# Chunked attention and a channel mixer: the first batch's front in another order, softmax by minima with exponentials from PSUM, v in fewer transfers

## The chip, the cores and the metric

The kernel runs on one core of a Trainium2 chip. The metric is the device time of one execution in microseconds (us), the median of three runs. The core has engines that run side by side, each through its own list of instructions in order: TensorE (PE, matmuls into PSUM; its weight loads are listed as PEld), VectorE (DVE), ScalarE (ACT), GpSimd (POOL), and SyncE (SP), whose queue issues all DMA transfers of this kernel. Semaphores make an instruction wait for one of another engine or for a transfer. SBUF is the working memory, PSUM holds the results of matmuls in eight banks of 128 x 512 floats.

## The reference

Four batches, 8 heads, 768 positions, head size 64. Attention runs over chunks of 32 queries, each with 8 memory keys and up to 56 keys around the chunk; a low-rank mix over the sequence and a two-layer feed-forward follow. All inputs are float32.

```python
for c in range(nc):                      # 24 chunks
    l_start, r_end = max(0, 32 * c - 16), min(S, 32 * c + 40)
    k_full = concat([mem_k, k[:, :, l_start:r_end]], axis=2)
    v_full = concat([mem_v, v[:, :, l_start:r_end]], axis=2)
    scores = scale * q_c @ k_full.T
    scores = scores - max(scores, axis=-1)
    a = exp(scores)
    a = a / (sum(a, axis=-1) + 1e-09)
    out[:, :, 32 * c:32 * c + 32] = a @ v_full
...
xt = x.transpose(0, 2, 1)                # x: out with the heads side by side, 768 x 512
h = xt @ U @ V                           # U 768 x 32, V 32 x 768
u = x + h.transpose(0, 2, 1)
return u + maximum(u @ w_ch1, 0) @ w_ch2 # 512 -> 2048 -> 512
```

## The kernel before

The weights U, V, w1 and w2 come as 64-bit floats and are read as pairs of words. A class `Words` turns them into a float32 value on the chip: `begin` (ScalarE, one instruction for each transferred half), `bits`, `low` and `join` (VectorE). A weight block f (16 of them, 128 hidden columns each) has two chunks, 2f for w1 and 2f+1 for w2. `finish` splits a chunk's value into a high part (a ScalarE copy, L322) and a low part (a VectorE subtraction, L323), since each product of the feed-forward runs as three matmul passes. The generator `stream` (L332) walks through all chunks; one call of `advance(1)` is one step of it: begin of the next chunk with bits of this one and finish of the one before, then low, then join.

Attention works in three steps T of 256 query positions (`NP` = 3). For each T:

- `regroup` (L398, VectorE) reorders raw k and q; `k_part` and `q_part` transpose them on PE and copy them to `kall` and `qt` (L472 to L480 and L492). `kall` holds the windows of two T, so k_part(2) writes the half of T=0 and the last edge of T=1.
- `s_turn` (L508) computes the scores of one T into two PSUM banks with 128 small matmuls.
- `s_weights` (L515) takes them out, for each bank: a memset for positions beyond the ends, a maximum over each window of 64 columns (L530), a subtraction into `pt` (L531), both on VectorE, and one exponential over 512 columns on ScalarE (L534).
- `s_sums` (L536) sums and inverts; `t_part` (L550) transposes the probabilities on PE and copies them out on ScalarE (L558); `av_part` (L560) multiplies with v and, on VectorE, with the inverse sums (L579), which gives x.

For batch 0 these parts are called in an order written out by hand in `attention` (from L601), with `collect` (x times U), `spread_v`, `turn_x` and calls of `advance` among them. In this front, PE, VectorE, ScalarE and SP all keep the order in which the code calls them (`manual_schedule`); `keep_clock` adds matmuls on zeros. PSUM banks are taken by `bank` in a fixed cycle of seven (`cyc`, L98), so the n-th request waits until the reader of the (n-7)-th is done. After the front, g (x times U, collected) is split (L780, L781), joined with V into u (`join_uT`, L824; `join_uT1`, L855), and the feed-forward begins: `both_blocks` (L946) runs the hidden blocks f of both halves of batch 0, while VectorE still decodes weights; it needs chunks 2f and 2f+1 for block f. The attention of batches 1 to 3 is placed among the feed-forward of the batch before, there with `s_part` and the planner's order.

Loads follow a list, `LOADS`, all on the SP queue: `t` are k and q of one T (6 transfers for T=0, 4 each for the others), `mk` mem_k, `uv` U and V (4), `mv` mem_v into a small tile (2), `v0` to `v2` the windows of v of one T (8 transfers, of 56 rows and one head each, and 2 for the ends of the sequence), `mm` copies of the small tile into every window of all three homes (6), `w0` to `w2` three weight blocks (3 each).

```python
LOADS = 't0 mk t1 t2 uv mv v0 mm v1 w0 v2 w1 w2'
cyc = ["a", "h", "a", "o0", "a", "h", "o1"]
```

## Time and profile before

| | |
|---|---|
| median of 3 runs | 707.15 us (703.69, 707.15, 709.41) |
| the profiled execution | 707.29 us |
| its span, first to last instruction | 705.5 us |
| mean granted clock of PE | 0.973 |
| bytes moved by DMA | 79.35 MB |

In a table of stretches each row starts with the stretch in us and its length, then gives busy time and instructions of PE, PEld, DVE, ACT and POOL, the granted clock of PE (1.00 is full), the mean busy share of the 16 DMA engines and what they moved in GB/s. In a timeline a row gives start, duration, engine, line, operation, out<-in by the program's names, shapes, the number of instructions merged into the row, and in brackets the idle time before it with what ended it. Instructions that follow each other on one engine overlap in their durations, so the distance of two starts is what one costs. SPq rows are issues of transfers, not the transfers.

### The profile page before, as it was taken

The numbers are of one execution on the slowest core, as the hardware profiler recorded it, in microseconds if no ns is written. First come the engines' busy times: TensorE is split into PE (matmuls) and PEld (weight loads), VectorE is DVE, ScalarE is ACT, GpSimd is POOL, SyncE is SP. The second block draws the span as 40 slices with busy tenths as digits, with TensorE's granted clock in tenths as the row PEclk, the third lists the DMA queues.
The fourth block names the chain that finished last, engine by engine and source line by source line (L and its number), as shares of the span: only waits on it lengthen the run. The fifth ranks groups of instructions, "written<-read, shape, count | busy, mean of one in ns | idle before, by whom it ended". The sixth has DMA issues, their size and how long they took to land.

```text
span 705.5 us, 14740 instructions
## 1 busy us (share of the span) xinstructions
PE 670.0 (95%) x6284; PEld 583.1 (83%) x6284; DVE 319.1 (45%) x652; ACT 190.0 (27%) x470; POOL 10.1 (1%) x35
## 2 busy tenths in 40 slices
PE   7786999999977899999999999999999999999997
PEld 4465999998956489998988998898978999989996
DVE  5868989999673622316413222316313321112111
ACT  4534434333541113332211223222211211111110
POOL 2000000000000000000000000000000000000000
PEclk9997999999997789999999999999999999999999
DMA  8696444414453096412511178412411042214211
GB/s 228 158 279 234 149 150 150 155 45 131 129 143 111 33 231 170 110 41 89 131 32 61 31 220 197 121 46 88 128 34 59 32 129 65 60 31 134 74 47 45
DMA packets 103658, 79.35 MB, mean 112 GB/s; under 512 B 49480, under 2 KB 83400, under 8 KB 103592
## 3 DMA queue, kind: packets, MB, share of 16 engines
q1 hardware_dynamic: 103592, 78.40, 38.7%
q8 instruction: 49, 0.80, 0.5%
q14 instruction: 17, 0.14, 0.1%
HBM read 66.72 MB, written 10.49 MB: 109 GB/s over the span
## 4 chain that ended last, share of the span: by engine, by line
PE 85%; DVE 8%; DMA 2%; issue 2%; ACT 1%; SPq 1%; POOL 0%; DVEq 0%; ACTq 0%; POOLq 0%
PE ps_h L889 37%; PE acc L932 21%; PE acc L937 11%; PE ps_a L570 2%; PE ps_a L508 2%; PE ps_a L932 2%; PE ps_a L449 2%; DMA w1l<-w1ld 2%; PE ps_a L555 1%; PE acc L590 1%; PE ps_a L937 1%; DVE mx L530 1%; DVE pt L531 1%; PE ps_a L874 1%; PE ps_a L596 1%
## 5 line engine op out<-in xcount | busy, mean ns | idle before, releaser
L896 DVE SCALAR_TENSOR_TENSOR hl<-ps_h,hh 128x384 fp32r<-128x384 f32 x127 | 70.5, 556 | 252.1 <-ACT hh L895 251.4
L889 PE MATMUL ps_h<-uh,w1h 128*128 128x384 f32 x508 | 173.6, 343 | 8.0 <-ACT w1h L322 7.3
L889 PE MATMUL ps_h<-ul,w1h 128*128 128x384 f32 x508 | 172.3, 340 | 0.2 <-DVE ul L877 0.2
L932 PE MATMUL acc<-w,hh 128*128 128x512 f32 x594 | 156.4, 397 | 0.8 <-DVE x L903 0.8
L895 ACT ACTIVATE hh<-ps_h 128x384 fp32r<-128x384 f32 x127 | 62.5, 492 | 304.7 <-PE ps_h L889 304.7
L932 PEld LDWEIGHTS acc<-w,hh 128*128 128x128 f32 x594 | 109.2, 188 | 23.2 <-DVE x L903 1.2
L889 PE MATMUL ps_h<-uh,w1l 128*128 128x384 f32 x508 | 111.7, 341 | 1.7 <-DMA w1l<-w1ld 1.7
L889 PEld LDWEIGHTS ps_h<-uh,w1h 128*128 128x128 f32 x508 | 96.3, 190 | 13.5 <-ACT w1h L322 8.0
L889 PEld LDWEIGHTS ps_h<-ul,w1h 128*128 128x128 f32 x508 | 96.6, 190 | 3.0 <-DVE ul L877 0.7
L889 PEld LDWEIGHTS ps_h<-uh,w1l 128*128 128x128 f32 x508 | 92.1, 192 | 3.1 <-DMA w1l<-w1ld 2.3
L937 PE MATMUL acc<-w,hl 128*128 128x512 f32 x297 | 84.4, 391 | 0.0
L937 PEld LDWEIGHTS acc<-w,hl 128*128 128x128 f32 x297 | 55.7, 188 | 11.9
L932 PE MATMUL acc<-w2last,hh 128*128 128x512 f32 x90 | 25.7, 413 | 0.0
L794 DVE TENSOR_TENSOR x<-ps_a,x 128x512 f32<-128x512 f32 x24 | 15.6, 686 | 22.1 <-PE ps_a L792 22.1
L472 ACT COPY kall<-ps_a 128x256 f32<-128x256 f32 x40 | 16.9, 422 | 26.5 <-PE ps_a L449 26.5
L903 DVE TENSOR_TENSOR x<-acc,x 128x512 f32<-128x512 f32 x24 | 15.5, 685 | 18.2 <-PE acc L937 14.4
L508 PE MATMUL ps_a<-kall,qt 64*32 64x64 f32 x1344 | 19.4, 224 | 3.8 <-issue 3.5
L508 PEld LDWEIGHTS ps_a<-kall,qt 64*32 64x32 f32 x1344 | 16.8, 105 | 7.2 <-issue 6.6
L534 ACT ACTIVATE pt<-pt 128x512 f32<-128x512 f32 x24 | 14.6, 630 | 26.3 <-DVE pt L531 26.3
L932 PEld LDWEIGHTS acc<-w2last,hh 128*128 128x128 f32 x90 | 17.3, 198 | 3.9 <-issue 0.8
L194 DVE SCALAR_TENSOR_TENSOR vb<-vb 128x512 int32<-128x512 int32 x29 | 20.1, 692 | 0.9
L210 DVE TENSOR_TENSOR vb<-vb 128x512 f32<-128x512 f32 x29 | 20.0, 691 | 0.8
(186 smaller groups left out, 639.2 us busy)
## 6 DMA issues: line engine op xcount, KB each, us to landing
w1l<-w1ld SPq DMA_DIRECT2D x99, 256.0 KB
rw<-in_moe_w_ch_dram SPq DMA_DIRECT2D x14, 512.0 KB
qraw<-in_q_dram SPq DMA_DIRECT2D x24, 256.0 KB
out_dram<-x SPq DMA_DIRECT2D x24, 256.0 KB
vb<-in_v_dram SPq DMA_DIRECT2D x56, 98.0 KB
raw<-in_moe_w_ch_dram SPq DMA_DIRECT2D x20, 256.0 KB
kraw<-in_k_dram SPq DMA_DIRECT2D x16, 256.0 KB
rw<-in_moe_w_ch_dram SPq DMA_DIRECT2D x16, 256.0 KB
```

The source lines that it names most:

```text
L194: nc.vector.scalar_tensor_tensor(out=ti, in0=yi, scalar=-2 ** 31, in1=ti, op0=ALU.bitwise_and, op1=ALU.bitwise_or,)
L210: self.adder.tensor_tensor(out=t, in0=t, in1=y, op=ALU.add)
L472: copy(out=kt[:, p, :, :, m:m + w], in_=psv[:, q_])
L508: nc.tensor.matmul(out=psv[s][CK * i:CK * i + CK, t, p % 2, p // 2, :], lhsT=qt[p // 2][rows, p % 2, NI * t + i, :], rhs=kall[rows, NB * ( ...
L534: nc.scalar.activation(out=pt, in_=pt, func=AF.Exp, scale=scale)
L794: nc.vector.tensor_tensor(out=x, in0=hp, in1=x, op=ALU.add)
L889: nc.tensor.matmul(out=ph[:, :TOK], lhsT=w[:, c, :], rhs=u[c], start=(m == 0), stop=(m + 1 == len(parts)),)
L895: nc.scalar.activation(out=hh, in_=ph[:, :TOK], func=AF.Relu)
L896: nc.vector.scalar_tensor_tensor(out=hl, in0=ph[:, :TOK], scalar=0.0, in1=hh.bitcast(F32), op0=ALU.max, op1=ALU.subtract,)
L903: nc.vector.tensor_tensor(out=x, in0=bank, in1=x, op=ALU.add)
L932: nc.tensor.matmul(out=acc[tt], lhsT=h[:, sl], rhs=w, start=(begins and m == 0), stop=False,)
L937: nc.tensor.matmul(out=acc[tt], lhsT=hl[:, sl], rhs=w2h[f], start=False, stop=ends is not None)
```

## The change

The sign of the scores is turned: q is copied with a factor of -scale, so the memory holds negative scaled scores. `s_weights` becomes `s_min` (memsets with +3e38 and a minimum for each window, on VectorE) and `s_exp`: for each of the 8 windows of a bank one exponential straight from PSUM, exp(min - score), with the minimum as the bias operand. The subtraction on VectorE is gone, and the bank is held until the exponentials have read it. This holds for all batches.

In the front of batch 0, U's begin and a first `advance(1)` come ahead of k_part(2); U's other steps, the exponentials, the sums and the transposes move to later places, each `s_exp` behind other work; steps of the weight stream are spread over the front, 8 in all where there were 5. V's words get a home of their own instead of one of the three scratch pairs.

The homes of v for T=0 and 1 become one tile of 16 windows. `load_v_span` loads it with one transfer for each head and half (15 windows instead of 7 and 8), 10 transfers where there were 18; the copies of mem_v fill all windows of a tile in one transfer for each half. In the list of loads, mem_v moves ahead of t1, and w0 ahead of all of v.

```diff
-LOADS = 't0 mk t1 t2 uv mv v0 mm v1 w0 v2 w1 w2'
+LOADS = 't0 mk mv t1 t2 uv m0 w0 va m1 vb w1 w2'
...
-    vbs = [const.tile([P, NB, 4 * D], F32, name=f"vb{n}") for n in range(2)]
+    vb01 = const.tile([P, 2 * NB, 4 * D], F32, name="vb01")
+    vbs = [vb01[:, NB * n:NB * n + NB] for n in range(2)]
...
+                for j in range(4):
+                    rows = vv[b, g, CK * n0 - LEFT:CK * n0 - LEFT + NW - NM, j]
+                    step, count = rows.ap[0]
+                    nc.sync.dma_start(
+                        out=home[r0:r0 + NW - NM, n0 - m0:n1 - m0, D * j:D * j + D],
+                        in_=bass.AP(rows.tensor, rows.offset, [[step, count], [CK * step, n1 - n0], rows.ap[1]]),
+                    )
...
-                (nc.vector.tensor_copy if b == 0 and T == 0 else nc.scalar.copy)(
-                    out=qt[:, q_].rearrange("c i (n r) -> c r i n", r=2), in_=psv[:, q_],
-                )
+                to, src = qt[:, q_].rearrange("c i (n r) -> c r i n", r=2), psv[:, q_]
+                if b == 0 and T == 0:
+                    nc.vector.tensor_scalar(out=to, in0=src, scalar1=-scale, scalar2=None, op0=ALU.mult)
+                else:
+                    nc.scalar.mul(out=to, in_=src, mul=-scale)
...
-                nc.vector.tensor_reduce(out=mx, in_=sc, axis=AX.X, op=ALU.max)
-                nc.vector.tensor_tensor(
-                    out=ptv, in0=sc, in1=mx[:, :, None].broadcast_to([P, 8, NW]), op=ALU.subtract,
-                )
-                nc.scalar.activation(out=pt, in_=pt, func=AF.Exp, scale=scale)
+                nc.vector.tensor_reduce(out=mn, in_=sc, axis=AX.X, op=ALU.min)
+                mins[T, s] = sc, mn
+
+        def s_exp(T, s):
...
+            for a in range(8):
+                nc.scalar.activation(
+                    out=pt[:, NW * a:NW * a + NW], in_=sc[:, a], func=AF.Exp, bias=mn[:, a:a + 1], scale=-1.0,
+                )
```

The order of batch 0's front after the change, from the first scores on (each line ends at a `yield`):

```python
keep_clock(GAP[0]); sc = s_turn(0); q_part(1, *); s_min(0, *sc)
regroup(qraw, qn, "qn", 2); u_words.begin(); advance(1); k_part(2, *); u_words: bits, low, join; s_exp(0, *)
keep_clock(GAP[1]); sc = s_turn(1); q_part(2, *); s_min(1, *sc); s_sums(0); t_part(0, *)
s_exp(1, *); advance(2); sc = s_turn(2); s_min(2, *sc)
keep_clock(GAP[2]); v_words.begin(); s_sums(1); t_part(1, *); s_exp(2, *); advance(1); av_part(0); v_words: bits, low, join; collect(0, 1)
t_part(2, *); av_part(1); s_sums(2); spread_v; collect(2, 3); turn_x; advance(1)
keep_clock(GAP[3]); av_part(2); advance(3); keep_clock(CHAIN[0]); collect(4, 5); turn_x1 twice
```

Before, it was:

```python
keep_clock(GAP[0]); sc = s_turn(0); q_part(1, *); s_weights(0, *sc)
regroup(qraw, qn, "qn", 2); k_part(2, *); s_sums(0); t_part(0, *)
keep_clock(GAP[1]); sc = s_turn(1); q_part(2, *); s_weights(1, *sc)
sc = s_turn(2); u_words: begin, bits, low, join; t_part(1, *); s_weights(2, *sc); s_sums(1)
keep_clock(GAP[2]); av_part(0); v_words: begin, bits, low, join; s_sums(2); t_part(2, *); collect(0, 1)
av_part(1); spread_v; advance(1); collect(2, 3); turn_x; advance(3)
keep_clock(GAP[3]); av_part(2); advance(1); keep_clock(CHAIN[0]); collect(4, 5); turn_x1 twice
```

More of the change, by code (lines that the diff above doesn't have):

```diff
@@ L17 @@
 U32 = mybir.dt.uint32
-NEG = -3.0e38
+FAR = 3.0e38
 NSLOT = 23
@@ L183, in begin @@
                 return
-            self.y, self.t = work_pair()
+            if self.home is None:
+                self.y, self.t = work_pair()
+            else:
+                both = const.tile([P, 2, 256], F32, name="dec", tag=self.home)
+                self.y, self.t = both[:, 0, :], both[:, 1, :]
             for raw, c in self.pieces():
@@ L546, in s_part @@
         def s_part(T):
-            s_weights(T, *s_turn(T))
+            s_min(T, *s_turn(T))
+            for s in range(2):
+                s_exp(T, s)
             s_sums(T)
@@ L652, in attention @@
                 q_part(1, h)
-            s_weights(0, *sc)
+            s_min(0, *sc)
             yield
             regroup(qraw, qn, "qn", 2)
+            u_words.begin()
+            advance(1)
             for h in two:
                 k_part(2, h)
-            s_sums(0)
-            for s in two:
-                t_part(0, s)
-            yield
-            keep_clock(GAP[1])
-            sc = s_turn(1)
-            for h in two:
-                q_part(2, h)
-            s_weights(1, *sc)
-            yield
-            sc = s_turn(2)
-            u_words.begin()
             u_words.bits()
@@ L677, in attention @@
             for s in two:
-                t_part(1, s)
-            s_weights(2, *sc)
-            s_sums(1)
+                s_exp(0, s)
+            yield
+            keep_clock(GAP[1])
+            sc = s_turn(1)
+            for h in two:
+                q_part(2, h)
+            s_min(1, *sc)
+            s_sums(0)
+            for s in two:
+                t_part(0, s)
+            yield
+            for s in two:
+                s_exp(1, s)
+            advance(2)
+            sc = s_turn(2)
+            s_min(2, *sc)
             yield
             keep_clock(GAP[2])
+            v_words.begin()
+            s_sums(1)
+            for s in two:
+                t_part(1, s)
+            for s in two:
+                s_exp(2, s)
+            advance(1)
             av_part(0)
-            v_words.begin()
             v_words.bits()
@@ L687, in attention @@
             val = v_words.join()
-            s_sums(2)
-            for s in two:
-                t_part(2, s)
             for t in two:
@@ L693, in attention @@
             yield
+            for s in two:
+                t_part(2, s)
             av_part(1)
+            s_sums(2)
             spread_v(val)
-            advance(1)
             for t in two:
@@ L700, in attention @@
             early = turn_x()
-            advance(3)
+            advance(1)
             yield
@@ L704, in attention @@
             av_part(2)
-            advance(1)
+            advance(3)
             keep_clock(CHAIN[0])
@@ L721, in attention @@
                 clear_v()
-                for home in vbs[:2]:
-                    mem_v(home)
+                mem_v(vb01)
             yield
@@ L742, in attention @@
                         clear_v()
-                        for home in vbs[:2]:
-                            mem_v(home)
+                        mem_v(vb01)
                         yield
```

55 lines of the change are left out of this document (37 added, 18 removed).

## The prediction

> **What bounds the kernel now.** I read the page first (span and shares), then the table of stretches, one for each stage: PE, weight loads, VectorE, ScalarE, POOL busy, then granted clock, DMA share, GB/s.
>
> ```profile
> span 705.5 us, 14740 instructions
> PE 670.0 (95%) x6284; PEld 583.1 (83%) x6284; DVE 319.1 (45%) x652; ACT 190.0 (27%) x470; POOL 10.1 (1%) x35
> ...
> 0.00:62.00 62.00, 43.72 (x940) 29.58 (x941) 45.73 (x108) 27.84 (x79) 4.88 (x19) 0.93 0.81 234
> 62.00:176.00 114.00, 113.68 (x567) 103.02 (x565) 105.04 (x207) 45.50 (x96) 0.00 (x0) 0.98 0.41 132
> 260.00:705.00 445.00, 440.05 (x3736) 393.21 (x3736) 122.09 (x240) 89.90 (x219) 2.63 (x8) 1.00 0.32 88
> ```
>
> The profiled execution took 707.29 us, 1.8 more than its span and 0.1 above the median of 707.15. From 62 to 176 PE is busy 113.7 of 114 us, from 260 on 440 of 445. So the front, up to the first matmuls of f=1 at 60.78, is a lump that everything behind it follows: a front shorter by x is worth x. VectorE decodes weights beside PE until 176 (105 of 114 us busy), nearly as full, so it cannot repay a late start either.
>
> Next the chain of waits, the timeline of VectorE, ScalarE and the SP queue, for the front.
>
> ```profile
> 18.59 0.43 PE ps_a L116 x2
> 20.64 0.68 DVE mx L530
> 60.78 4.21 PE ps_h L889 x12
> ...
> 15.13 0.69 ACT L492 COPY qt<-ps_a 128x256 f32<-128x256 f32 x2
> 17.25 0.63 ACT L534 ACTIVATE pt<-pt 128x512 f32<-128x512 f32 x1 [0.92 <-DVE pt L531]
> 17.79 0.38 ACT L472 COPY kall<-ps_h 128x256 f32<-128x256 f32 x1
> 18.69 0.24 ACT L476 COPY kall<-ps_h 128x48 f32<-128x48 f32 x1
> 18.78 0.26 ACT L480 COPY kall<-tail 128x32 f32<-128x32 f32 x1
> 20.03 0.68 ACT L558 COPY pt<-ps_a 128x512 f32<-128x512 f32 x1
> 43.54 0.44 ACT L186 ACTIVATE dec<-rw 128x256 f32<-128x256 f32 x1 [2.14 <-DMA rw<-in_moe_w_ch_dram]
> 44.23 0.43 ACT L186 ACTIVATE dec<-raw 128x256 f32<-128x256 f32 x1 [0.24 <-DMA raw<-in_moe_w_ch_dram]
> ...
> 22.67 0.69 DVE L531 TENSOR_TENSOR pt<-acc,mx 128x512 f32<-128x512 f32 x1
> 29.73 1.27 DVE L539 TENSOR_REDUCE rs<-pt 128x8 f32<-128x512 f32 x2
> 39.70 0.41 DVE L579 TENSOR_TENSOR x<-ps_h,rs 128x256 f32<-128x256 f32 x1
> 46.04 1.42 DVE L579 TENSOR_TENSOR x<-ps_a,rs 128x256 f32<-128x256 f32 x4 [1.63 <-PE ps_a L570]
> 49.24 0.42 DVE L781 TENSOR_TENSOR g<-acc,g 32x256 fp32r<-32x256 f32 x1
> 54.17 0.42 DVE L200 TENSOR_SCALAR dec<-dec 128x512 int32<-128x512 int32 x1
> 57.62 0.55 DVE L896 SCALAR_TENSOR_TENSOR hl<-ps_a,hh 128x384 fp32r<-128x384 f32 x1
> ...
> 11.14 2.22 SPq L226 DMA_DIRECT2D vraw<-in_moe_V_dram  x3
> 13.40 0.68 SPq L620 DMA_DIRECT2D mv<-in_mem_v_dram  x2
> 19.55 3.04 SPq L413 DMA_DIRECT2D vb<-mv  x4
> 30.56 0.45 SPq L281 DMA_DIRECT2D rw<-in_moe_w_ch_dram  x1
> 40.32 0.82 SPq L281 DMA_DIRECT2D rw<-in_moe_w_ch_dram  x1
> 41.18 0.46 SPq L281 DMA_DIRECT2D raw<-in_moe_w_ch_dram  x1
> ```
>
> Two places matter. Scores, subtraction and exp wait for each other on VectorE and ScalarE from 14 to 32. And behind the joined u (54.17) VectorE decodes 3.45 us for chunk 1 and 2, then 0.55 for hl, then chunk 2 again, while PE stands idle until 60.78.
>
> **The change part by part.**
>
> Subtractions. Six in the front at 0.69 us (22.67): VectorE is freed of 4.1 us, 1.4 in each score step.
>
> Exponentials. Each 512-column exp becomes eight of 64 columns with a bias per partition. No row has that operand. Low bound: the 512-column exp starts 17.25 and the next instruction 17.79, 0.54; the 48-column copy lets the next one start 0.09 later (18.69, 18.78), so 464 columns fewer cost 0.40 less than a 512-column copy's 0.49 and a 64-column exp takes about 0.13. High bound: no overlap at all, the 0.26 of the 32-column copy. I take 0.15, near the exp's own row. Sixteen make 2.4 us of ScalarE where 1.1 stood, 48 make 7.2 for 3.2: ScalarE gains 4.0 (3.0 to 9.3). [...]
>
> mem_v ahead. Its two loads move from 13.40 to before the loads of t1, 0.68 of SP issue. The queue is full there (DMA share 1.04 in the table below), so the k of T=1 comes 0 to 0.7 later; I take 0.3.
>
> First weights ahead, and the wait they bring. SP now ends the loads of V at 13.4+0.3. Then two copies of mv over 16 blocks instead of 8: 0.76 each (3.04/4) if the size is free, 1.5 if not; I take 1.0, so w0 is issued at 15.7 and its second half at 16.2. From issue to use such a half took 43.54-40.32 = 3.2 and 44.23-41.18 = 3.05 us. So it is there at 19.2 (18.3 to 20.5). In the new order ScalarE runs u's first step and then `advance(1)`, the begin of chunk 0, before the copies of k_part(2) and before the exponentials. It gets there at 16.4 (the q copies of T=1 end 15.13+0.69 = 15.8, 0.3 later now, 0.3 for u) and stands 2.8 us. Behind it on the same engine: 0.43 for the second half, twelve copies (17.79 to 20.03, 2.24), eight exps (1.2), which free the bank that s_turn(1) needs (seven banks in turn). Sum 19.2+0.43+2.24+1.2 = 23.1. s_turn(1) takes 1.6 (from the warming matmuls' end at 19.02 to its reader at 20.64) and ends at 24.7: 4.1 late.
>
> Making it up. VectorE's part of T=1 and 2 is shorter by 2.8, but ScalarE is the bound now: the q copies wait for s_turn(1) and their transposes until 25.6 and take 1.1, two pT copies 1.0, sixteen exps 2.4, which brings 30.1; s_turn(2) starts at half of those, 28.9, and ends at 30.5; minima with their memsets 1.7, sums 1.7 (1.27 and two small steps), join 0.7, four products 1.4 give x of T=0 at 36. Then two collects 2.0, two pT 1.1, av 1.45 and products 1.4: x of T=1 ends near 41.5 against 40.1. Collects, 24 transposes, av(2) and products follow as before: x of T=2 ends at 49.0 against 47.4 (46.04+1.42), 1.6 late.
>
> Decode ahead. Eight steps of the stream run before "joined" instead of five. Chunk 0's bits, low part and join (3.0 us) now lie where VectorE waits. But `advance(3)` puts low, join, bits and rest of chunk 1 (3.45, the block from 54.17 to 57.62) between x and g: g starts at 49.0+3.45 = 52.5 instead of 49.24. From g to the end of ul is 54.17-49.24 = 4.9, so 57.4 against 54.17. Then hl (its matmuls and relu first, 1.8), low and join of chunk 2 (1.9) and the w1h copy with its wait 0.7: f=1 starts at 61.8 to 62.3. I take 62.3, 1.5 late.
>
> v in fewer transfers.
>
> ```profile
> 15.00:20.00 5.00, 3.58 (x123) 2.67 (x123) 4.44 (x10) 4.08 (x17) 0.00 (x0) 1.00 0.68 155
> 30.00:35.00 5.00, 3.46 (x8) 1.23 (x8) 4.79 (x14) 1.86 (x4) 0.00 (x0) 0.74 0.80 205
> ```
>
> Ten issues fewer, the same bytes, hidden: v moves behind w0, and av(0) needs all of va (15 blocks of 56 rows of 256 B, eight times, 1.7 MB). At the 155 to 205 GB/s of two stretches of v loads, from 19 on, that is 27 to 30; av(0) comes at 32. If that cover goes, each us late is a us. vb has until 46, w1 until 42. The multiplication by -scale rides on copies of the same size, the sentinel and the tile for V's words change no time: 0.
>
> The clock. In windows of 3.41 us:
>
> ```profile
> 5.07:8.48 3.41, 3.18 (x22) 2.16 (x20) 1.28 (x3) 2.15 (x10) 0.00 (x0) 1.00 1.04 287
> 8.48:11.90 3.42, 1.72 (x10) 1.00 (x10) 2.59 (x9) 1.86 (x10) 0.00 (x0) 1.00 1.07 317
> 28.97:32.38 3.41, 1.50 (x9) 1.06 (x10) 3.31 (x10) 2.01 (x4) 0.00 (x0) 1.00 0.72 157
> 32.38:35.79 3.41, 3.41 (x17) 0.73 (x24) 3.27 (x9) 0.00 (x0) 0.00 (x0) 0.50 0.90 264
> 63.10:66.51 3.41, 3.41 (x14) 3.41 (x14) 2.57 (x5) 1.70 (x3) 0.00 (x0) 0.50 0.94 303
> 66.51:69.92 3.41, 3.41 (x22) 3.12 (x21) 2.40 (x6) 1.73 (x5) 0.00 (x0) 1.00 0.07 26
> 213.28:216.70 3.42, 1.42 (x103) 1.38 (x102) 0.68 (x3) 0.00 (x0) 0.40 (x1) 1.00 0.75 259
> 233.76:237.18 3.42, 1.33 (x4) 0.24 (x2) 0.68 (x1) 1.17 (x2) 0.00 (x0) 1.00 0.00 0
> ```
>
> A window with PE busy 1.50 or less is followed by half clock, one with 1.72 is not; full clock returns after a full window (63.10, then 66.51). [...] PE, idle from 17.2 to 23.0 in my schedule, has one whole window empty, well under 1.50 busy, so s_turn(1) and what follows run at half clock. Its four steps between (s_turn, q, pT, s_turn, some 5 us) cost up to 2.9 where PE ends last, nothing where ScalarE does: I take 1.5. At f=1 the idle time shrinks from 6.5 to some 4 us; half clock from 60.78 to 66.51 cost 2.9, I take back 1.0 (0 to 1.4).
>
> Batches 1 to 3. The exps cost ScalarE 1.3 us more per step. From 260 on the waits of PE are one line:
>
> ```profile
> PE ps_h L889 <- DMA w1l<-w1ld: 1.7, 2, 1.0
> ```
>
> ScalarE is busy 90 of 445 us there, and no transpose of the probabilities waits for it. Cover: PE has the feed-forward to do. Without it each of nine steps would cost 1.3, less 1.4 of VectorE. Batch 1 around 195 to 250 has little cover, but the two nearly cancel: 0 (-1 to +1).
>
> Sum: +1.5 (f=1 later) +1.5 (half clock early) -1.0 (less of it at f=1) +0 = +2.0; 707.3+2.0 = **709.3 us**.
>
> **The rivals.**
>
> *Slower by over 1%.* ScalarE as the front's bound with the clock low throughout. Place: 17 to 58. If one exp takes 0.25, near its high bound (+2.1), and PE, always waiting a little for ScalarE, never fills a window before g, its 8 us of transposes, av and collects on the path run twice as long, +4 more. 709.3+6.1 = 715. It decides from 0.2 per exp with half clock beyond 30. For it: no row excludes that price. Against: collects at 32.38 filled a window at once.
>
> *Faster.* The half clocks of batch 1 (two windows, 1.42 and 1.33 busy) hang on where windows fall. Idle time there is 2 to 3 us; moved by half a window it parts into two windows above 1.72 each. Both gone returns some 10 us: 699. For it: three runs differ by 5.7. Against: all lie above 703.
>
> *It changes nothing.* w0 lands before ScalarE asks (copies of mv at 0.7, half 2.8) and exps cost 0.13: f=1 at 60, cold a little less, 705.5. For it: bounds from rows. Against: even then issue at 15.2 plus 3.05 is 18.2, after 16.4.
>
> **How the numbers follow.** Forecast (706.5 to 713) 0.52, slower rival 0.20, faster 0.13, nothing (703 to 706.5) 0.15. 1%, about what a measurement can tell here, is 7.1 us: under 700.1 only the faster rival, 0.13; over 714.2 the slower, 0.20; between 0.67. The range 701 to 716 leaves out the better part of the faster rival and the tail of the slower one.
>
> **What would show it.** Right: ScalarE idle for about 2.8 us before the second begin of chunk 0, released by the DMA of w0; s_turn(1) after 23; half clock in the twenties; no VectorE decode of chunk 1 behind ul; f=1 at 61 to 64. Wrong: begin of chunk 0 without a wait, 64-column exps 0.2 apart or more, av(0) released by a v transfer, f=1 before 60, or a second half clock missing in batch 1.

## The result and the profile after

| | before | after |
|---|---|---|
| median of 20 runs each | 707.27 us | 712.57 us |
| lowest and highest | 703.69 to 711.97 us | 707.34 to 716.51 us |
| after : before | | 1.0073, 95% interval 1.0053 to 1.0094 |
| span of the profiled execution | 705.5 us | 710.3 us |

The kernel became slower by 5.3 us: by less than one per cent, and more than the measurement's error. First the head of the page and the sums by engine, as the changed kernel has them.

```profile
span 710.3 us, 14864 instructions
PE 674.2 (95%) x6284; PEld 585.7 (82%) x6284; DVE 304.8 (43%) x628; ACT 215.3 (30%) x638; POOL 10.6 (1%) x35
```

VectorE gave up 14 us and ScalarE took on 25, as the exchange of a subtraction for seven more exponentials says; PE stays the bound. Where the span grew is read by cutting both executions at the same points of the work. The cuts here are the starts of the 4th, 28th, 37th, 65th, 73rd and 91st Relu of the feed-forward on ScalarE. Table of stretches of the kernel before, without its second row and its last:

```profile
0.00:76.03 76.03, 57.75 (x1006) 42.61 (x1007) 57.69 (x130) 34.13 (x92) 4.88 (x19) 0.91 0.76 220
...
180.26:267.26 87.00, 75.74 (x1060) 59.84 (x1059) 42.58 (x91) 27.95 (x82) 2.62 (x8) 0.86 0.50 135
267.26:409.56 142.30, 142.30 (x1475) 126.36 (x1474) 46.98 (x95) 33.48 (x83) 2.02 (x6) 1.00 0.28 78
409.56:445.56 36.00, 34.96 (x192) 31.84 (x191) 7.53 (x17) 10.18 (x34) 0.00 (x0) 1.00 0.83 208
445.56:539.88 94.32, 94.32 (x1217) 82.45 (x1216) 33.37 (x71) 22.79 (x54) 0.61 (x2) 1.00 0.28 81
```

And the same work in the changed kernel:

```profile
0.00:81.42 81.42, 60.39 (x1006) 44.41 (x1007) 53.93 (x124) 40.10 (x135) 4.85 (x19) 0.90 0.73 205
...
185.66:268.20 82.54, 74.42 (x1060) 58.82 (x1059) 39.76 (x85) 34.37 (x124) 2.02 (x6) 0.88 0.52 136
268.20:411.19 142.99, 142.76 (x1475) 126.52 (x1474) 43.09 (x89) 39.94 (x124) 2.02 (x6) 1.00 0.29 81
411.19:449.26 38.07, 36.02 (x187) 32.62 (x186) 7.53 (x17) 9.44 (x33) 0.00 (x0) 0.96 0.79 197
449.26:544.99 95.73, 95.73 (x1222) 83.28 (x1221) 29.48 (x65) 29.96 (x97) 0.61 (x2) 1.00 0.28 80
```

Call them A (the front), B (the attention of batch 1), the long one, C (the loads of batch 2) and D. A grew by 5.4 us, B shrank by 4.5, the long one, C and D grew by 0.7, 2.1 and 1.4; the stretches left out are equal or 0.3 shorter. That is the 4.8 us of the span. In these two executions the front lost what the whole lost, and behind it a gain and a loss of four to five us cancel. Of B's gain 3.1 us are idle time of PE (11.3 us before, 8.1 after), the rest is work at a higher clock (75.74 and 74.42). One execution of each is little to go by: the twenty runs of one kernel lie 8 to 9 us apart, so a few us in a stretch are shown only where other runs repeat them.

The front, in the timeline of the changed kernel:

```profile
13.73 1.66 SPq L418 DMA_DIRECT2D vb<-mv  x2
15.43 1.60 SPq L286 DMA_DIRECT2D rw<-in_moe_w_ch_dram  x1
17.09 2.50 SPq L286 DMA_DIRECT2D raw<-in_moe_w_ch_dram  x1
...
15.49 0.38 ACT L191 ACTIVATE dec<-uarea 128x192 f32<-128x192 f32 x1 [0.26 <-DMA uarea<-in_moe_U_dram]
21.70 0.43 ACT L191 ACTIVATE dec<-rw 128x256 f32<-128x256 f32 x1 [5.84 <-DMA rw<-in_moe_w_ch_dram]
22.49 0.43 ACT L191 ACTIVATE dec<-raw 128x256 f32<-128x256 f32 x1 [0.36 <-DMA raw<-in_moe_w_ch_dram]
22.83 0.35 ACT L500 COPY kall<-ps_h 128x256 f32<-128x256 f32 x1
25.07 1.82 ACT L567 ACTIVATE pt<-ps_h,mn 128x64 f32<-128x64 f32 x8
26.65 0.44 ACT L567 ACTIVATE pt<-ps_a,mn 128x64 f32<-128x64 f32 x1
...
24.01 0.31 PE L538 MATMUL ps_h<-kall,qt 64*32 64x64 f32 x1 [8.09 <-ACT kall L504]
66.36 1.65 PE L936 MATMUL ps_h<-uh,w1h 128*128 128x384 f32 x4 [3.68 <-ACT w1h L327]
...
37.95 0.42 DVE L616 TENSOR_TENSOR x<-ps_a,rs 128x256 f32<-128x256 f32 x1
45.01 0.42 DVE L616 TENSOR_TENSOR x<-ps_h,rs 128x256 f32<-128x256 f32 x1
52.77 1.42 DVE L616 TENSOR_TENSOR x<-ps_a,rs 128x256 f32<-128x256 f32 x4 [2.78 <-PE ps_a L607]
54.11 0.42 DVE L205 TENSOR_SCALAR dec<-dec 128x512 int32<-128x512 int32 x1
57.67 0.42 DVE L828 TENSOR_TENSOR g<-acc,g 32x256 fp32r<-32x256 f32 x1
```

ScalarE finishes U's begin at 15.9 and then stands 5.84 us for w0, and 0.36 for its second half. Everything behind it waits in order: the copies of k_part(2) from 22.83, and for these PE, which stands 8.09 us and goes on with s_turn(1) at 24.01, ahead of the exponentials from 25.07; in the kernel before, its warming matmuls ended at 19.02 and s_turn(1) followed at once. One exponential follows the next after (26.65-25.07)/8 = 0.197 us. f=1 starts at 66.36 instead of 60.78.

Why w0 is late is seen in the landings, which the profiler records as semaphore events of each transfer (us; worked out from the trace):

```
kernel, transfer                           issued   landed   between
before  copies of mv, 64 KB, first two      19.55    22.82      3.27
                                            20.44    23.94      3.50
after   copies of mv, 128 KB, both          13.73    19.04      5.31
                                            14.69    21.44      6.75
after   w0, the two halves of w1's block    15.43    21.68      6.25
                                            17.09    22.47      5.38
after   last part of v for T=0 and 1        31.06    35.90      4.84
```

w0's halves land right behind the two copies, 5.4 to 6.3 us after issue instead of about 3.1. Part of this is SP itself: the two issues last 1.60 and 2.50 us, where the same two take 0.45 and 0.46 in the kernel before, and 1.58 and 0.47 in the first experiment, which has no copies in front of them. So the copies go with the standing of the second; what holds SP is not shown. And v, which is behind w0, is complete at 35.9 and not between 27 and 30.

The clock, in stretches of 3.41 us, and one of 5 us for the transfers. In the two traces, before and after, the stretches at half clock lasted 3.41, 6.83, 10.24 or 13.65 us, but for one that the end of each execution cuts off (worked out from the trace); a window is a stretch of 3.41 us on that grid.

```profile
15.00:20.00 5.00, 0.92 (x7) 0.32 (x5) 2.97 (x9) 0.61 (x2) 0.35 (x1) 1.00 0.61 94
17.02:20.43 3.41, 0.00 (x0) 0.00 (x0) 1.05 (x3) 0.00 (x0) 0.35 (x1) 1.00 0.72 113
20.43:23.84 3.41, 0.00 (x0) 0.00 (x0) 0.00 (x0) 1.78 (x8) 0.00 (x0) 0.50 0.97 289
23.84:27.25 3.41, 3.24 (x132) 3.07 (x133) 1.02 (x2) 3.41 (x21) 0.40 (x1) 0.50 0.60 94
426.62:430.03 3.41, 1.38 (x8) 1.30 (x9) 1.70 (x5) 0.38 (x1) 0.00 (x0) 1.00 0.75 146
430.03:433.44 3.41, 3.41 (x11) 2.92 (x10) 0.56 (x1) 0.69 (x3) 0.00 (x0) 0.50 0.94 239
44.32:47.73 3.41, 3.29 (x10) 1.21 (x5) 3.31 (x10) 2.06 (x6) 0.00 (x0) 0.50 0.96 333
```

PE does nothing from 17.02 to 23.84, and the clock is at half until 27.25, over all of s_turn(1) that was left; a window from 44.32, with collects and transposes of x, is at half clock too. In stretch C a window with 1.38 us of work is followed by one at half clock; the kernel before has none in C. From 15 to 20 us the transfers move 94 GB/s with the engines 0.61 busy; in the kernel before it was 155. In the trace the first copy of mv, to 8 partitions, raised its semaphore in 9 steps, from 15.00 to 19.04 us, and the first half of w0, to 128 partitions, in 16, from 20.50 to 21.68.

### The profile page after: what moved, and what is told of

The parts are those of the page before. It is cut to its first block, busy times and chain, and to the rows that moved or that the text cites. A ratio compares the mean times of both kernels' runs of the same rounds, so it can differ in the third digit from the quotient of the medians.

```text
span 710.3 us, 14864 instructions
## 1 busy us (share of the span) xinstructions
PE 674.2 (95%) x6284; PEld 585.7 (82%) x6284; DVE 304.8 (43%) x628; ACT 215.3 (30%) x638; POOL 10.6 (1%) x35
## 3 DMA queue, kind: packets, MB, share of 16 engines
q1 hardware_dynamic: 103416, 78.40, 38.7%
## 4 chain that ended last, share of the span: by engine, by line
PE 83%; DVE 5%; DMA 4%; SPq 4%; ACT 1%; issue 1%; DVEq 0%; ACTq 0%
PE ps_h L936 36%; PE acc L979 21%; PE acc L984 10%; DMA w1l<-w1ld 3%; PE ps_a L607 2%; PE ps_a L979 2%; PE ps_a L538 2%; PE ps_a L477 2%; SPq L440 1%; PE ps_a L592 1%; PE ps_a L984 1%; PE ps_a L633 1%; PE ps_a L921 1%; PE acc L627 1%; DVE x L841 1%
## 5 line engine op out<-in xcount | busy, mean ns | idle before, releaser
L979 PE MATMUL acc<-w,hh 128*128 128x512 f32 x594 | 158.4, 401 | 0.3 <-DVE x L950 0.3
L567 ACT ACTIVATE pt<-ps_a,mn 128x64 f32<-128x64 f32 x168 | 36.4, 389 | 17.8 <-DVE mn L555 15.4
L574 DVE TENSOR_REDUCE rs<-pt 128x8 f32<-128x512 f32 x24 | 16.3, 686 | 15.6 <-ACT pt L567 15.6
L616 DVE TENSOR_TENSOR x<-ps_a,rs 128x256 f32<-128x256 f32 x44 | 15.7, 410 | 11.2 <-PE ps_a L607 7.4
```

Of the source, the lines that this page charges most:

```text
L567: nc.scalar.activation(out=pt[:, NW * a:NW * a + NW], in_=sc[:, a], func=AF.Exp, bias=mn[:, a:a + 1], scale=-1.0,)
L574: nc.vector.tensor_reduce(out=rs[:, :, :, :, s].rearrange("n t g k -> n t k g"), in_=pts[T, s].rearrange("n (t k g w) -> n t k g w", t=2, ...
L616: nc.vector.tensor_tensor(out=x[:, 4 * D * g:4 * D * g + 4 * D].rearrange("n (j d) -> n j d", d=D), in0=psv[g][:, t], in1=rs[:, t, g].rear ...
L979: nc.tensor.matmul(out=acc[tt], lhsT=h[:, sl], rhs=w, start=(begins and m == 0), stop=False,)
```

## The experiments

Each kernel was timed in five rounds beside the kernel before on the same chip. The table gives the ratio of its time to that of the kernel before with the interval, the start of f=1 and the lengths of A, B, C and D in its profiled execution (us). One execution was profiled of each, so these lengths carry the scatter of one run; that of the loads alone was the fastest of its twelve (707.68 us, their median 711.50).

| kernel | ratio | interval | f=1 | A | B | C | D |
|---|---|---|---|---|---|---|---|
| before | 1 | | 60.78 | 76.03 | 87.00 | 36.00 | 94.32 |
| after | 1.0073 | 1.0053 to 1.0094 | 66.36 | 81.42 | 82.54 | 38.07 | 95.73 |
| w0 ahead of the copies | 1.0053 | 1.0030 to 1.0076 | 62.43 | 76.61 | 85.63 | 38.53 | 95.70 |
| begin later | 1.0076 | 1.0050 to 1.0102 | 64.29 | 78.48 | 85.70 | 38.71 | 95.70 |
| one exponential | 1.0069 | 1.0042 to 1.0095 | 67.97 | 82.47 | 81.00 | 35.89 | 95.58 |
| before, loads alone | 1.0040 | 1.0013 to 1.0068 | 64.76 | 78.72 | 81.41 | 37.13 | 94.43 |
| before, softmax alone | 0.9982 | 0.9961 to 1.0003 | 61.34 | 76.61 | 85.05 | 35.56 | 94.43 |
| steps as before | 1.0104 | 1.0081 to 1.0127 | 66.14 | 80.17 | 87.12 | 36.18 | 95.81 |
| same, v ahead of w0 | 1.0041 | 1.0018 to 1.0064 | 61.49 | 75.72 | 86.69 | 37.75 | 95.70 |
| small copies later | 1.0026 | 0.9995 to 1.0056 | 66.74 | 80.71 | 85.15 | 35.66 | 95.58 |
| front rebuilt | 0.9981 | 0.9957 to 1.0005 | 61.59 | 76.87 | 83.16 | 35.89 | 94.35 |
| same, v by T | 0.9958 | 0.9924 to 0.9991 | 64.44 | 78.97 | 79.08 | 36.19 | 94.46 |
| same, av(2) earlier | 0.9952 | 0.9926 to 0.9978 | 62.49 | 77.01 | 79.56 | 38.55 | 95.65 |
| same, v of T=1 ahead of w0 | 0.9898 | 0.9873 to 0.9923 | 60.59 | 74.67 | 78.34 | 35.55 | 95.61 |

### w0 ahead of the copies

```diff
-LOADS = 't0 mk mv t1 t2 uv m0 w0 va m1 vb w1 w2'
+LOADS = 't0 mk mv t1 t2 uv w0 m0 va m1 vb w1 w2'
```

> The changed kernel with the first weights w0 loaded ahead of the two 16-block copies of mem_v instead of behind them; nothing else moves. Theory (ScalarE stands for w0, and w0 stands behind the copies): w0's halves are issued at about 13.7 and 14.5 and are there by 18, ScalarE's two waits for them shrink from 5.84+0.36 to under 2.5 us, s_turn(1) ends near 22.5 instead of 26.05, f=1 starts 2 to 4 us earlier than 66.36, and the time is 0.997 to 1.004 of the kernel before (after: 1.0073). Rival A (the eight small exponentials and the half clock carry the loss): the waits shrink but f=1 stays within 1 us of 66.4, ratio 1.006 to 1.009. Rival B (the transfers are only full: whatever is behind the copies comes late): the copies land later, v with them, av(0) waits for v by 2 us or more, ratio 1.005 or more.

ScalarE's timeline of this run:

```profile
18.32 0.44 ACT L191 ACTIVATE dec<-rw 128x256 f32<-128x256 f32 x1 [1.99 <-DMA rw<-in_moe_w_ch_dram]
18.99 0.43 ACT L191 ACTIVATE dec<-raw 128x256 f32<-128x256 f32 x1 [0.24 <-DMA raw<-in_moe_w_ch_dram]
```

The waits fell from 6.2 to 2.2 us, s_turn(1) ended at 22.3 and f=1 came 3.9 us earlier, as the theory had it: the copies held w0. Of the front's 5.4 us all but 0.6 was gone. PE stood 1.2 us for v, less than rival B asked. The ratio stayed above the theory's range, at 1.0053; in the profiled execution B was 3.1 us longer than in the changed kernel, and the timing does not tell the two kernels apart.

### The begin later on ScalarE

```diff
             u_words.begin()
-            advance(1)
...
             for s in two:
                 s_exp(0, s)
+            advance(1)
             yield
```

> The changed kernel with ScalarE's first step of the weight stream put behind the copies of k_part(2) and the exponentials of T=0 instead of ahead of them; loads and the number of steps unchanged. Theory (order on ScalarE): k_part(2) and the exponentials no longer wait for w0, s_turn(1) ends by 21 instead of 26.05, f=1 starts 3 to 5 us earlier than 66.36, ratio to the kernel before 0.996 to 1.003. Rival A (exponentials and clock): ratio 1.006 to 1.009. Rival C (the wait only moves: ScalarE now stands for w0 ahead of the q copies of T=2 and the exponentials of T=1, or av(0) stands for v that lands at 28 to 36 anyway): x of T=0 not before 36, f=1 within 1.5 us of 66.4, ratio 1.005 to 1.008.

PE's waits from 12 to 46 us (in total, times, longest):

```profile
PE ps_a L607 <- DMA vb<-in_v_dram: 3.3, 4, 1.0
PE ps_a L592 <- ACT pt L567: 1.9, 1, 1.9
PE ps_a L607 <- DVE dec L215: 1.6, 1, 1.6
```

s_turn(1) ended at 19.2, seven us earlier than in the changed kernel, and x of T=0 came at 38.5, no earlier at all: av(0) began at 28.6 and went on to 37.1, since it stood again and again for parts of v, at half clock between (0.31 us a matmul at 30.64, as at 24.01 in the changed kernel, and 0.22 there at 36.71, at full clock). (The 1.6 us put down to a step of the decoding are v's too: that step ends at 30.1, a part of v landed at 30.47, and PE went on at 30.56.) This is rival C in its place and its ratio: behind the wait for w0 stood the wait for v. That f=1 came 2.1 us earlier is more than the 1.5 that it allowed. It was won later: x of T=1 came 0.4 us earlier, x of T=2 1.6, and between them the changed kernel has its collects and transposes at half clock.

### One exponential again

```diff
                 nc.vector.tensor_reduce(out=mn, in_=sc, axis=AX.X, op=ALU.min)
-                mins[T, s] = sc, mn
+                nc.vector.tensor_tensor(out=pt..., in0=sc, in1=mn[:, :, None]..., op=ALU.subtract)
...
-            for a in range(8):
-                nc.scalar.activation(out=pt[...], in_=sc[:, a], func=AF.Exp, bias=mn[:, a:a + 1], scale=-1.0)
+            nc.scalar.activation(out=pt, in_=pt, func=AF.Exp, scale=-1.0)
```

> The changed kernel with the softmax of before (row extreme, subtraction on VectorE, one exponential of 512 columns) in the new order and with the new loads. Theory: ScalarE loses 0.8 to 1.0 us of exponentials per bank in the front (eight at 0.197 against one of about 0.5 to 0.6), VectorE gains 0.69 per bank; the wait for w0 stays 5 to 6 us, so f=1 moves by at most 1.5 us from 66.36 and the ratio to the kernel before is 1.004 to 1.009. Rival A (the eight exponentials are the cost): f=1 3 us or more earlier and ratio 1.000 to 1.003.

Ratio 1.0069, as the theory said: the eight exponentials are not the loss. f=1 came 1.6 us later, a little outside the expected 1.5; in that run ScalarE stood 7.45 us for w0, also more than the 5 to 6 expected.

### The softmax alone, in the kernel before

```diff
-                    out=qt[...], in_=psv[:, q_],
+                    nc.scalar.mul(out=to, in_=src, mul=-scale)
...
-                nc.vector.tensor_reduce(out=mx, in_=sc, axis=AX.X, op=ALU.max)
-                nc.vector.tensor_tensor(out=ptv, in0=sc, in1=mx[...], op=ALU.subtract)
-                nc.scalar.activation(out=pt, in_=pt, func=AF.Exp, scale=scale)
+                nc.vector.tensor_reduce(out=mn, in_=sc, axis=AX.X, op=ALU.min)
+            for a in range(8):
+                nc.scalar.activation(out=pt[...], in_=sc[:, a], func=AF.Exp, bias=mn[:, a:a + 1], scale=-1.0)
```

> The kernel before with only the softmax changed: minima instead of maxima, q multiplied by -scale, eight exponentials of 64 columns from PSUM in place of the subtraction and one of 512; loads and order are those of before. The four runs so far put part of the loss behind the front: between about 410 and 446 us the changed kernel, and it with w0 first or with the begin later, lose 2.1 to 2.7 us against the kernel before (a longer wait for w1l from DRAM and a window at half clock behind it), the one with one exponential loses nothing there. Theory (the softmax brings that): the same stretch loses 2 to 3 us here too, the front moves by less than 2 us, ratio 1.002 to 1.006. Rival (order of the instructions of the later batches, not the softmax): that stretch within 0.5 us, ratio 0.998 to 1.002.

The theory fell: C is 35.56 us, no longer than before, and the whole 0.9982, which is no change or a small gain. The exchange itself costs nothing that the timing shows. What the exponentials cost in a row is seen in ScalarE's timeline of this run, where nothing interrupts them:

```profile
15.18 1.77 ACT L539 ACTIVATE pt<-ps_h,mn 128x64 f32<-128x64 f32 x8
16.74 1.84 ACT L539 ACTIVATE pt<-ps_a,mn 128x64 f32<-128x64 f32 x8
```

(16.74-15.18)/8 = 0.195 us each, the same as in the changed kernel.

### The loads alone, in the kernel before

The list of loads, `load_v_span`, the joined home of v and `mem_v` as in the change; nothing else.

> The kernel before with only the transfers changed (mem_v ahead, its copies larger, w0 ahead of v, v in fewer transfers); the order on the engines and the softmax are those of before. Theory: w0's place costs nothing here, since ScalarE first asks for it after 40 us; what can cost is v behind it: av(0) at 26 has to wait for v that lands at 28 to 36, so x of T=0 ends up to 4 us later than 31.4 to 32.7, less what is made up behind it: ratio 1.000 to 1.005. Rival B (the transfers alone carry the loss): ratio 1.006 to 1.009. Nothing: 0.999 to 1.001 with av(0) not released by a v transfer.

PE's waits from 12 to 46 us in this run:

```profile
PE ps_a L594 <- DMA vb<-in_v_dram: 6.9, 5, 4.3
```

In the order of before, av(0) is ready at 26 and stands 6.9 us and a first 0.3 for v, 4.3 of them at once; f=1 comes 4.0 us later, and the whole is slower by 0.4%. Of the two parts of the change that ran alone this is the one that costs; the new order alone, with loads and softmax of before, was not run.

### The steps as before, and then v ahead of w0

First all steps of the weight stream where the kernel before has them, in the changed order; then also another list.

```diff
-LOADS = 't0 mk mv t1 t2 uv m0 w0 va m1 vb w1 w2'
+LOADS = 't0 mk mv t1 t2 uv m0 va m1 vb w0 w1 w2'
```

> The changed kernel with all steps of the weight stream where the kernel before has them (first begin behind the spread of V, three steps behind the transposes of x, one behind av(2)); loads unchanged. Theory (two waits stand one behind the other: w0 on ScalarE, and v, which lies behind w0 and the copies of mem_v): ScalarE no longer waits for w0, s_turn(1) ends by 20, but av(0) still stands for v that lands at 28 to 36, so x of T=0 ends at 37 to 38.5 as with the begin behind the exponentials; f=1 at 62 to 66, ratio 1.003 to 1.008. Rival (only w0 held it): x of T=0 by 33, f=1 before 60, ratio under 1.000.

> The same order as the run before it (steps of the weight stream as in the kernel before), and the loads of v, va, m1 and vb ahead of w0. Theory: with v no longer behind 1 MB of weights, va lands by 29 instead of 36, av(0) waits less than 1.5 us for it, x of T=0 ends at 31 to 33.5 and f=1 starts 5 us or more earlier than in the run before it (56 to 60); ratio to the kernel before 0.990 to 0.999. Rival (the copies of mem_v hold v, not w0): va still lands after 32, x of T=0 not before 35, ratio 1.000 to 1.005. Rival (w0 becomes the end: its decode starts only after 36): x of T=0 early, but f=1 not before 62, ratio 1.000 to 1.006.

With the steps alone, s_turn(1) ended at 18.9, av(0) began at 27.5 and ended at 36.7. Its longest stand, 3.24 us, is listed as "issue", but PE went on 0.09 us after a part of v had landed. Before f=1 PE stood 6.46 us where the changed kernel stood 3.68: the decode ahead is worth 2.8 us there. All fourteen traces agree: 6.5 us in the five kernels without it, 3.7 in the nine with it. This kernel has the highest ratio of all, though its A is 1.25 us shorter than the changed kernel's; B, at 87.12, has none of the gain.

With v ahead of w0, v of T=0 and 1 landed by 30.4, av(0) ended at 31.6, and A was 0.3 us shorter than in the kernel before. So the two waits together are the front's loss: both had to go. But f=1, at 61.49, came later than the 56 to 60 expected, and the ratio was still 1.0041, above the range: B was near its length of before, and C and D were 1.75 and 1.4 us longer. By the timing the mended front returns about 2.3 of the 5.3 us; the rest of the loss lies behind it.

### Small copies of mem_v in the later batches

Batches 1 to 3 copy mem_v too, and the change made four copies of 64 KB into two of 128 KB there as well.

```diff
-                mem_v(vb01)
+                for home in vbs[:2]:
+                    mem_v(home)
```

> The changed kernel with mem_v of batches 1 to 3 copied in four transfers of 8 blocks (64 KB) again, as before the change, in place of two of 16 blocks (128 KB); the front is untouched. Theory (the large copies hold the load of w1l that is queued behind them: in batch 2 it takes 8.06 us from issue to landing against 5.68 before): it takes 5 to 6.5 us, PE's wait for it near 428 falls from 2.05 to at most 1.2 us, the window at half clock behind it goes, the stretch from 410 to 446 (38.07 us) shrinks by 1 to 2.5 us, front unchanged (f=1 within 0.5 us of 66.4), ratio to the kernel before 1.003 to 1.006. Rival (the order of the instructions, or where the batch begins, brings that wait): the wait stays at 1.7 us or more, ratio 1.006 to 1.009.

PE's waits from 405 to 540 us, of the kernel before:

```profile
PE ps_h L889 <- DMA w1l<-w1ld: 1.0, 1, 1.0
```

of the changed kernel:

```profile
PE ps_h L936 <- DMA w1l<-w1ld: 2.1, 1, 2.1
```

and of this one:

```profile
PE ps_h L938 <- DMA w1l<-w1ld: 0.7, 1, 0.7
```

The wait for w1l fell below that of before, the window at half clock was gone (granted clock 1.00 from 425 to 431.8 us), and C went from 38.07 to 35.66 us with the front untouched (f=1 at 66.74). The ratio, 1.0026, is a little under the expected 1.003, and its interval just meets that of the changed kernel. The load of w1l behind the copies, by issue and landing in all fourteen traces:

```
large copies (7 kernels)   7.2 to 8.5 us   changed kernel 8.06
small copies (7 kernels)   3.7 to 6.4 us   before 5.68, this run 5.29
```

The two groups do not overlap, but this measure favours the small copies: four issues take 1.5 us longer than two, so the load behind them is issued later. Counted from the first copy's issue, the load had landed after 8.7 to 10.0 us with large copies and after 7.8 to 9.4 with small ones, 0.8 apart in the mean, and these ranges overlap. What parts the groups is SP's issue of that load: it lasted 1.5 to 2.1 us behind large copies and 0.4 to 0.5 behind small ones. What C makes of it depends on more. With large copies it was 35.9 to 38.7 us, with small ones 35.6 to 36.2, but once 38.55 (the run with av(2) earlier, 6.36 us for w1l, a wait of 2.0 and a half clock behind it). So the copies make the long wait likely. A half clock followed it in four of the seven with large copies; what decides that, no run shows.

### A front built from this

The last four kernels put together what the runs had shown. The first loads v ahead of mem_v's copies, w1 ahead of the rest of v, keeps the small copies in the later batches, and spreads eight steps of the weight stream where nothing waits behind ScalarE. Of its edit against the changed kernel:

```diff
-LOADS = 't0 mk mv t1 t2 uv m0 w0 va m1 vb w1 w2'
+LOADS = 't0 mk mv t1 t2 uv va m0 w0 w1 m1 vb w2'
...
             u_words.begin()
-            advance(1)
...
-            advance(2)
             sc = s_turn(2)
...
             val = v_words.join()
+            advance(3)
```

> The changed kernel with v ahead of the mem_v copies of the front and of all weights, w1 ahead of the last part of v, eight steps of the weight stream again but none on ScalarE ahead of the last exponentials (one behind them, three behind the join of V's words, one behind the spread, two behind the transposes of x, one behind av(2)), and mem_v of batches 1 to 3 in four copies. Theory (the two waits, for w0 and for v, are what the front lost, and the decode ahead is worth 3 us when it stands where VectorE is idle): av(0) waits less than 1 us, x of T=0 by 33, f=1 at 57 to 59 against 60.78 before and 61.49 with the steps as before; the whole 0.991 to 0.997 of the kernel before. Rival (decode ahead only moves between x and g): f=1 at 60 to 62, ratio 0.998 to 1.003. Rival (the copies of mem_v, now behind v, hold av(0)): av(0) waits 2 us or more for a vb that mv was copied to, f=1 after 60, ratio 1.000 to 1.004.

The ratio was 0.9981 and f=1 came at 61.59. Both fit the first rival's numbers (0.998 to 1.003, 60 to 62), but the place is the second rival's: av(0) stood 1.5 us for the copies, now last, and 2.0 us more with nothing named, which ended 0.09 us after the second copy had landed at 30.60.

Then v by T in two buffers again, as before the change, so that av(0) waits for its own part alone:

```diff
-LOADS = 't0 mk mv t1 t2 uv va m0 w0 w1 m1 vb w2'
+LOADS = 't0 mk mv t1 t2 uv v0 m0 w0 v1 m1 w1 m2 v2 w2'
```

> The rebuilt front, with v loaded by T again as in the kernel before (ten transfers for T=0, then mem_v's two small copies into that part, then w0, the part of T=1 with its copies, w1, the part of T=2, w2), in two separate buffers instead of one. Theory (av(0) needs only the part of T=0 and its two copies; the change made it wait for v and mem_v of T=0 and 1 together): that part is there by 25, av(0) starts when its probabilities are turned, near 27, without a wait of 0.5 us or more for a transfer; no window at half clock between 29 and 37; x of T=0 ends by 31 (34.4 in the rebuilt front before this), f=1 starts at 56 to 59 against 61.59; ratio to the kernel before 0.990 to 0.996. Rival (the twelve more issues and the order of transfers make the parts of T=1 or 2 late): av(1) or av(2) waits 1 us or more, f=1 at 59 to 61, ratio 0.996 to 1.000.

PE's waits of this run, 12 to 46 us:

```profile
PE ps_a L583 <- issue: 4.3, 1, 4.3
PE ps_a L583 <- DMA vb<-mv: 2.1, 1, 2.1
...
PE ps_h L583 <- DMA vb<-mv: 0.9, 1, 0.9
```

av(0) ran from 27.7 to 29.4 without a wait, as expected, and x of T=0 was there by 31. But av(1) stood 3 us for mem_v's copies, and then 4.3 us for nothing that the profile names, so f=1 came at 64.44, later than either side expected. The ratio is 0.9958; in the profiled execution it was won in B, with A 2.9 us longer than before.

Next av(2) was put ahead of the transposes of x:

```diff
-            early = turn_x()
-            advance(2)
...
             av_part(2)
-            advance(1)
+            early = turn_x()
+            advance(3)
```

> The same with av(2) ahead of the 24 transposes of x on PE, and three steps of the weight stream behind them instead of two ahead and one behind. Theory: x of T=2 is ready while PE transposes, so PE's idle 0.8 us ahead of the last collects goes and g starts 1 to 2.5 us earlier than in the run before; f=1 0.5 to 2 us earlier (55 to 58), ratio 0.988 to 0.996. Rival (v of T=2 is not there by 40): av(2) waits for its transfer by 1 us or more and nothing is won, ratio within 0.001 of the run before.

f=1 came 2 us earlier, but at 62.49 it is far from the 55 to 58 expected, and the ratio is the same within its interval; C fell into half clock again (38.55).

Last, v of T=1 and its copies went ahead of w0:

```diff
-LOADS = 't0 mk mv t1 t2 uv v0 m0 w0 v1 m1 w1 m2 v2 w2'
+LOADS = 't0 mk mv t1 t2 uv v0 m0 m1 v1 w0 w1 m2 v2 w2'
```

> The last run's kernel with the part of v for T=1 and both pairs of mem_v copies ahead of w0. In the two runs before, av(1) waited 2 to 3 us for mem_v's copies behind w0 and then stood 2.8 to 4.3 us more with nothing named, and half clock followed. Theory (the copies and v of T=1 behind w0 hold av(1)): they are there by 30, av(1) starts right behind its transposes near 33.5 without a wait for a transfer; ScalarE waits at most 1.5 us for w0 ahead of the copies of the probabilities of T=2; x of T=1 by 38 (43.46 in the run before), f=1 at 56 to 60 against 62.49; ratio to the kernel before 0.989 to 0.995. Rival (the unnamed stand is the cost, and comes again): av(1) still ends after 40, f=1 after 61, ratio 0.995 to 0.999. Rival (w0 is late now): ScalarE stands over 2 us for it, ratio 0.995 to 1.000.

PE's waits from 30 to 45 us in this one:

```profile
PE ps_a L583 <- issue: 5.6, 1, 5.6
```

The waits for transfers are gone from av(1), and the stand that nothing names took their place, 5.6 us long: the rival for the front, though f=1, at 60.59, lies between its range and the theory's. Even so A is the shortest of all, and with B at 78.34 us the kernel takes 0.9898 of the time before (0.9873 to 0.9923), 700.55 us against 707.71 in those runs. It beats both kernels. Of the 10 us in A and B, 8.7 are B's, and the stretches behind take 2.4 back. B in this run:

```profile
178.90:257.24 78.34, 69.97 (x1060) 55.38 (x1059) 39.55 (x85) 34.58 (x124) 2.02 (x6) 0.93 0.54 142
```

PE's work in it is 69.97 us against 75.74 before, at a granted clock of 0.93 against 0.86, and its idle time 8.4 against 11.3. Why B is shorter was not isolated.

## Why the prediction was right, and where it was not

The forecast was no change within 1%, with 2.0 us lost; 5.3 were lost. The path was the one described: ScalarE stands for w0, PE behind it, s_turn(1) after 23, half clock in the twenties, a block of decoding between x and g, f=1 later. But f=1, at 66.36, lies outside its 61 to 64, and one of its own signs of being wrong came: parts of v released av(0), twice, for 0.7 us in all. That the total still fell within the range has two pieces of luck, named below at s_turn(1) and at batches 1 to 3. Point by point:

- **mem_v ahead.** 0.3 us were taken for k of T=1. None is seen: its first two loads landed at 8.27 and 9.08 us, before at 8.91 and 9.67, and s_turn(0) starts at 11.81, before at 12.40, and between 11.6 and 12.8 in the others.
- **The wait for w0** is the term that was mis-sized. "From issue to use such a half took" 3.2 us came from rows without a copy of mem_v in front; behind the two copies it took 6.3 and 5.4 (15.43 to 21.70, 17.09 to 22.49). The copies' issue was bounded, their transfer was not costed at all. 2.8 us were expected, 6.2 measured.
- **The exponentials**: 0.15 us each were taken, within bounds of 0.13 and 0.26; 0.197 were measured. Sixteen cost 0.75 us more than reckoned. The low bound was drawn too low: 448 columns fewer at 0.40 us for 464 leave 0.15 of the 0.54, not 0.13. That the price is not what the front lost is shown by the run with one exponential.
- **s_turn(1)** ended at 26.05 against 24.7 forecast, and here an error hid another. ScalarE was done with w0 3.3 us later than reckoned (22.92 against 19.63). But the sum puts all twelve copies and eight exponentials behind that, 3.4 us, and s_turn(1) went on 1.1 us behind it, after a part of the copies and ahead of every exponential: no bank held it. So it went on 0.9 us late, and half clock added 0.4 (24.01 to 26.05 is 2.0 us, where 1.6 were taken). With it x of T=0 was 2.4 us later than forecast (38.4 against 36), T=1 3.9 (45.4 against 41.5) and T=2 5.2 (54.2 against 49.0): av(1) stood 1.72 us near its end for nothing named, and collects and transposes ran at half clock from 44.3 to 47.7; the forecast had no term for either. (By its own terms x of T=1 comes to 41.95, not 41.5.) PE's waits of the changed kernel from 12 to 46 us, of which two bear on this and on v:

```profile
PE ps_a L607 <- issue: 1.7, 1, 1.7
...
PE ps_a L607 <- DMA vb<-in_v_dram: 0.7, 2, 0.5
```

- **v hidden.** "That is 27 to 30; av(0) comes at 32" was wrong in its first half: v is complete at 35.9. In the changed kernel this cost 0.7 us of waiting, since PE itself was late, but the cover was gone for every kernel that mended the first wait: 4.9 us with the begin later, 7.2 in the order of before. The estimate took the rate of v's loads from 19 us on, with the copies and a megabyte of w0 in front of them.
- **The decode ahead** went as costed: the block between x and g took 3.56 us (54.11 to 57.67) against 3.45, and from g to f=1 8.7 us against 9.8.
- **The clock** of the early front: one empty window was foreseen, two came, and half clock from 20.43 to 27.25. At f=1 1.0 us was to be taken back; half clock lasted from 66.4 to 71.6 there, 5.3 us against 5.7 before, which is 0.2.
- **Batches 1 to 3** were put at zero, and their sum is -0.6 us, but not because nothing happened: B -4.5, the long one +0.7, C +2.1, D +1.4. That they cancel in these two executions is luck, and what made B shorter is open. "No transpose of the probabilities waits" was true and beside the point. What the forecast overlooked is that the change also makes mem_v's copies larger there; that the run with small copies shows as C's loss in the changed kernel. D's goes with an order: the twelve collects of one step ran in one go before (first row, the kernel before) and were parted by a matmul in the changed kernel:

```profile
526.01 1.91 PE L596 MATMUL ps_a<-x,u_sb 128*32 128x512 f32 x12
```

```profile
529.94 1.90 PE L633 MATMUL ps_a<-x,u_sb 128*32 128x512 f32 x10
531.78 0.45 PE L936 MATMUL ps_h<-uh,w1h 128*128 128x384 f32 x1
532.15 1.05 PE L633 MATMUL ps_a<-x,u_sb 128*32 128x512 f32 x2
```

All fourteen traces divide so: D is 94.3 to 94.5 us in the five with twelve in one go, and 95.6 to 95.8 in the nine with a parting, 1.1 to 1.5 more. The kernel with one exponential has it, the kernels before with softmax or loads alone do not; why the later batches' order changed was not tried.

The rival "slower by over 1%" had its place right and its price wrong: it was to decide from 0.2 us per exponential and half clock beyond 30, and the exponentials came to 0.197 with half clock from 44.3 to 47.7 only, up to f=1. Its sum was off as well: 0.10 more for each of the 16 to 24 exponentials on the path is 1.6 to 2.4 us, so its 2.1 fits neither count, and 8 us that run twice as long cost 8, not 4. "It changes nothing" fell with w0. The rival "faster", by batch 1's half clocks, did not come for the changed kernel, but its place was well chosen: B varied from 78.3 to 87.1 us over the kernels, and the granted clock in it from 0.94 to 0.86. The three with v by T in the rebuilt front have it below 80; what sets it was not isolated.

## What to carry to other kernels

When an engine that runs in order is given an early step on data that is still loading, cost it by where its transfer stands in the queue, transfers that are slow for their size included (here 128 KB to 8 partitions, 5.3 and 6.8 us from issue to landing), and ask in the same breath which transfer was queued behind it: here the second wait hid behind the first, and with the first mended on ScalarE x of T=0 came no earlier. Joining transfers saved ten issues here, but made the first user wait for the last user's bytes: in the rebuilt front av(0) stood 1.5 and 2.0 us until copies into the joined home had landed, and with v by T not at all. Count a transfer's delay from a point that both kernels share, since what stands ahead of its issue moves too. And compare executions cut at the same points of the work: a front that lost all of it and later stages that cancelled looked, in the total, like one small loss.

## What the runs showed of the hardware that was not expected

**PE stood with its data landed, and a transfer of instructions ended shortly before it went on.** In seven traces PE stops in av(1) after 118 to 121 of 128 small matmuls, with all of its v landed, and goes on with nothing named as releaser: 1.23 us before, 1.72 after, 2.1 with the small copies later, 1.6 to 5.6 in the four rebuilt fronts. The view of the transfers shows an entry of another kind. The last kernel from 30.6 to 37.2 us has data alone:

```profile
q1 hardware_dynamic: 2240, 1.79, 95.9%
```

and from 37.2 to 39.8 us, the end of the stand:

```profile
q1 hardware_dynamic: 626, 0.16, 29.1%
q8 instruction: 1, 0.02, 2.7%
```

One packet of 16 KB for instructions starts at 37.22, lasts 1.14 us, and PE goes on at 39.78; the share of the data's transfers is 95.9% ahead of 37.2 us and 29.1% behind it. In the six others the same packet ends 1.2 to 1.6 us before PE goes on (before: 36.99 and 38.33; after: 42.12 and 43.65). "Issue" alone does not tell this: the two such stands at the start of av(0), 3.24 and 1.98 us, ended with the landing of data. That PE waits for the packet, and that the data's transfers hold the packet back, are the author's readings of these times; no run took either away.

**Fewer, larger copies were no faster in sum.** In batch 2 mem_v's four copies of 64 KB were done 7.2 us after the first one's issue in the kernel before, the two of 128 KB 8.3 us in the changed one; over all fourteen traces it is 6.5 to 8.0 against 7.7 to 8.7. SP's issue of the load behind them took 0.50 and 1.90 us. Why was not tried.

**The clock** went to half behind windows in which PE was partly busy: 1.38 us of 3.41 in stretch C. The busy time does not settle where the limit lies: in the changed kernel the window from 208.16 us has PE busy for 2.20 us and half clock follows, while the one from 201.33 has 2.03 and full clock follows. So the prediction's line, 1.50 or less against 1.72, holds in the kernel before and not in the changed one.
